# Hedgehog attention with a GLU: the attention coefficients of slabs 1 to 3 spread over the features by DMAs through DRAM

The change calls the four slabs 1 to 4; this text counts them from 0, as the code does. "Slabs 1 to 3" are the second to the fourth.

## The chip, the cores and the metric

The kernel runs on one core of a Trainium2 chip. The core has a matrix engine (TensorE, PE in the profile, with its weight loads shown as PEld), a vector engine (VectorE, DVE), an engine for functions of one input (ScalarE, ACT), a general one (GpSimd, POOL) and SyncE (SP), which here only issues DMAs. The metric is the device time of one execution, in microseconds.

## The reference

The input is one sequence of 2048 tokens with 512 features. Two layers of the same weights follow one another, each a linear attention and a GLU, with a layernorm before and a residual after each. All is bfloat16.

```python
def _A_ref(x, wqkv, w_phi, wo):          # H = 32 heads, Dh = 16
    q, k, v = ...                        # from x @ wqkv, per head
    pq = jnp.einsum("bhsd,hdf->bhsf", q, w_phi)
    pk = jnp.einsum("bhsd,hdf->bhsf", k, w_phi)
    phi_q = jnp.concatenate([_softmax(pq, axis=-1), _softmax(-pq, axis=-1)], axis=-1)
    phi_k = jnp.concatenate([_softmax(pk, axis=-1), _softmax(-pk, axis=-1)], axis=-1)
    kv = jnp.einsum("bhsf,bhsd->bhfd", phi_k, v)
    z  = jnp.einsum("bhsf->bhf", phi_k)
    num = jnp.einsum("bhqf,bhfd->bhqd", phi_q, kv)
    den = jnp.einsum("bhqf,bhf->bhq", phi_q, z)[..., None] + 1e-6
    return (num / den) ... @ wo

def _B_ref(x, W_gate, W_up, W_down):     # F = 1376
    gate = x @ W_gate
    return (gate * (gate > 0) * (x @ W_up)) @ W_down

for _ in range(2):
    x = x + _A_ref(_layernorm(x), A_wqkv, A_w_phi, A_wo)
    x = x + _B_ref(_layernorm(x), B_W_gate, B_W_up, B_W_down)
```

## The kernel before

The 2048 tokens are worked in four slabs of 512 (st = 0 to 3), each of four tiles of 128. x stays in on-chip memory as x_sb for the whole run. Queries, keys and what follows from them lie with features on the 128 partitions and the slab's 512 tokens along the free axis. The 512 query features make four chunks c of 128 (8 heads of 16), and each chunk exists for two signs sg, exp(pq) and exp(-pq): eight pieces of 128 x 512 per slab, in expq.

into_a is a layernorm and the keys of a slab (lines 425 to 512). Per tile it makes the exponentials of the keys (expk), their sums per head (L486, L488) and, on POOL, the values weighted by them (vhat, L495). expk and vhat have NE buffers, one per tile. The sums over tokens (kvsum, matmuls with expk and vhat) of a slab run after its four tiles: each sum reads all four buffers. In the first stage the four slabs' into_a follow one another; later into_a(st) follows glu(st), for the next layer.

out_of_a is queries, attend and a layernorm. The two softmaxes of a query and the division by the denominator come down to one coefficient per token, head and sign. attend(st) computes it in these steps:

- 32 small matmuls (L550, bank zd) give per token, head and sign the sum of the exponentials and its part of the denominator.
- ACT copies the sums out (Zs, L553), DVE multiplies and adds (zm L555, zden L557), ACT takes the reciprocal by a logarithm and an exponential (L558, L559), and DVE makes the coefficients atok (L561), with tokens on the partitions.
- PE transposes atok (L565) and DVE copies the result to aT (L566): 64 rows, one for each head and sign, with 512 tokens.
- Per chunk and sign, a matmul of aT with the 0/1 matrix EC (L570) spreads 8 rows of aT over 128 partitions, each row 16 times, into a PSUM bank. DVE multiplies expq by it: for sg = 0 straight from PSUM (L578), for sg = 1 after ACT has copied it to absb (L574, then L575). VIA chooses between the two.
- Two matmuls per chunk (L582) give the attention's output, ACT copies it to oT (L583), 16 matmuls with wo_sb project it (L588) and residual adds the result to x_sb (L592).

glu(st) (L594) has 88 matmuls for gate and up, and 44 with Wd; ACT takes the ReLU (L607), DVE multiplies (L609) into hT, which has NH slots; one glu holds 11 of them until its last tile is projected.

The order written in the code is, per layer: sums(); out_of_a(0); then for st = 0 to 3: out_of_a(st + 1), glu(st), and into_a(st) or, in the second layer, four output stores (L648).

That is not the order in which the engines run it. Program.schedule (L119) is a planner that runs at build time. Each operation has an engine, a cost occ (how long it holds its engine) and a latency lat. The planner takes the operation that can start first by these costs, and of several the one written first. The result is one fixed list per engine; a semaphore wait stands before an operation where it needs another engine's result. On the chip nothing is reordered: when an operation's input is late, all that is behind it on its engine waits.

A DMA is planned by these lines: it holds its issuer for 0.56 us on SP, all DMAs share one transfer line of 270 bytes per ns, and a fixed latency lies partly before and partly after.

```python
DMA_LAT = 1800.0
DMA_BW = 270.0
...
begin = max(s + 0.35 * self.DMA_LAT, qfree)
qfree = begin + o.nbytes / self.DMA_BW
o.finish = qfree + 0.65 * self.DMA_LAT
```

So nbytes, given with each DMA, sets only its planned time; what is moved is set by the access patterns. Operations with port=True (L575 and the layernorm's apply L449) are planned not to overlap with POOL's arithmetic.

Before the change the only DMAs after the loads at the start are the 16 output stores. They wait for one another, since all write the resource "out".

Of the kernel before, what the change touches and what calls it, by code (L numbers as in the profile page):

```python
# [7 lines left out]
BF16 = mybir.dt.bfloat16  # L8
I32 = mybir.dt.int32
ALU = mybir.AluOpType  # L10
ACT = mybir.ActivationFunctionType
# [47 lines left out]
class Program:  # L59
# [10 lines left out]
    def op(self, eng, fn, reads=(), writes=(), occ=100.0, lat=None, name="", bonus=0.0, port=False):  # L70
        o = Op(len(self.ops), eng, fn, reads, writes, occ, occ + 100.0 if lat is None else lat, name)
        o.bonus, o.port = bonus, port
        self.ops.append(o)
        return o
# [172 lines left out]
def build_kernel(nc, A_x, A_wqkv, A_w_phi, A_wo, W_gate, W_up, W_down, out):  # L247
# [8 lines left out]
    with ExitStack() as ctx:  # L256
# [4 lines left out]
        def sb(name, shape, dt=BF16):  # L261
            return E(nc.sbuf_tensor(name, [P] + list(shape), dt))

        NWARM = 8
        NY, NYT, NE, NV, NG, NH, NA = 4, 6, 6, 4, 3, 19, 3
        x_sb = sb("x_sb", [NT, 512])
        ytile = sb("ytile", [NY, 512])
        yT = sb("yT", [NYT, NC, 512])
# [33 lines left out]
        ident = sb("ident", [128])  # L302
        mask8a = sb("mask8a", [8])
        mask8 = sb("mask8", [8])
        absb = sb("absb", [NA, 512])
        pb = [E(nc.psum_tensor(f"pb{i}", [P, 512], FP32)) for i in range(8)]

        made = {}
# [1 line left out]
        def R(*key):  # L310
            if key not in made:
                made[key] = Res(str(key))
            return made[key]
# [3 lines left out]
        def bank(name):  # L317
            return Bank(name, pb)

        def mm(ps, view, lhsT, rhs, start, stop, reads, n, name):  # L320
            lat = 0.4167 * n + 167
            op("pe", lambda e: e.matmul(view(ps), lhsT, rhs, start=start, stop=stop),  # L322
               reads=reads, writes=[ps], occ=max(25.0, 0.4167 * n + 2.6), lat=lat, name=name)
# [5 lines left out]
        def full(ps):  # L329
            return ps.f32()  # L330

        def b16half(ps):
            return ps.b16()[:, 0:512]
# [85 lines left out]

        fold("k", Wknat, Wkp)  # L420

        cnt = {"y": 0, "yT": 0, "e": 0, "h": 0, "g": 0, "v": 0, "a": 0}
        VIA = lambda st, c, sg: sg == 1

        def layernorm(st, step=4, early=False):

# [112 lines left out]
        def attend(st):  # L539

            g = st % 2
            zd = bank(f"zd{st}")

            def zdv(p):
                return p.f32().rearrange("p (t q s h) -> p t q s h", t=4, q=2, s=2)

            for tt in range(4):
                for sg in range(2):
                    for c in range(NC):
                        mm(zd, (lambda tt, sg, c: lambda p: zdv(p)[:, tt, :, sg, c * 8:(c + 1) * 8])(tt, sg, c),  # L550
                           expq[:, st, c, sg, tt * 128:(tt + 1) * 128], ZDw[:, sg, c, :].rearrange("p (q h) -> p q h", q=2), True, True,
                           [R("eq", st, c, sg), R("ZDw", sg, c), R("ZDw1")], 16, f"zd{st}")
            op("act", lambda e: e.activation(Zs[:, g], zdv(zd)[:, :, 0], ACT.Copy), reads=[zd], writes=[R("Zs", g)], occ=270, lat=400, name="Zs")  # L553
            for s in range(2):
                op("dve", (lambda s: lambda e: e.tensor_tensor(zm[:, g, :, s, :], zdv(zd)[:, :, 1, s], Zs[:, g, :, 1 - s, :], ALU.mult))(s),  # L555
                   reads=[zd, R("Zs", g)], writes=[R("zm", g, s)], occ=200, lat=290, name="zm")
            op("dve", lambda e: e.tensor_tensor(zden[:, g], zm[:, g, :, 0, :], zm[:, g, :, 1, :], ALU.add), reads=[R("zm", g, 0), R("zm", g, 1)], writes=[R("zden", g)], occ=200, lat=290, name="zden")  # L557
            op("act", lambda e: e.activation(zr[:, g], zden[:, g], ACT.Ln), reads=[R("zden", g), R("tables")], writes=[R("zr", g)], occ=200, lat=300, name="zln")  # L558
            op("act", lambda e: e.activation(zr[:, g], zr[:, g], ACT.Exp, scale=-1.0), reads=[R("zr", g)], writes=[R("zr", g)], occ=200, lat=300, name="zr")  # L559
            for s in range(2):  # L560
                op("dve", (lambda s: lambda e: e.tensor_tensor(atok[:, g, :, s * 32:(s + 1) * 32], Zs[:, g, :, 1 - s, :], zr[:, g], ALU.mult))(s),  # L561
                   reads=[R("Zs", g), R("zr", g)], writes=[R("atok", g)], occ=195, lat=290, name="atok")
            pa = bank(f"aT{st}")
            for tt in range(4):
                tr(pa, (lambda tt: lambda p: p.b16()[:, tt * 128:(tt + 1) * 128])(tt), atok[:, g, tt, :], [R("atok", g)], f"aTt{st}")  # L565
            op("dve", lambda e: e.tensor_copy(aT[:, g, :], b16half(pa)), reads=[pa], writes=[R("aT", g)], occ=328, lat=415, name="aT")  # L566
            for c in range(NC):
                for sg in range(2):
                    ps = bank(f"ab{st}{c}{sg}")
                    mm(ps, full, EC[:, sg * 4 + c, :], aT[:, g, :], True, True, [R("EC"), R("aT", g)], 512, f"ab{st}")  # L570
                    if VIA(st, c, sg):
                        ab = cnt["a"] % NA
                        cnt["a"] += 1
                        op("act", (lambda ab, ps: lambda e: e.activation(absb[:, ab, :], full(ps), ACT.Copy))(ab, ps), reads=[ps], writes=[R("absb", ab)], occ=480, lat=610, name=f"abc{st}")  # L574
                        op("dve", (lambda c, sg, ab: lambda e: e.tensor_tensor(expq[:, st, c, sg, :], expq[:, st, c, sg, :], absb[:, ab, :], ALU.mult))(c, sg, ab),  # L575
                           reads=[R("eq", st, c, sg), R("absb", ab)], writes=[R("eq", st, c, sg)], occ=335, lat=420, name=f"em{st}", port=True)
                    else:
                        op("dve", (lambda c, sg, ps: lambda e: e.tensor_tensor(expq[:, st, c, sg, :], expq[:, st, c, sg, :], full(ps), ALU.mult))(c, sg, ps),  # L578
                           reads=[R("eq", st, c, sg), ps], writes=[R("eq", st, c, sg)], occ=595, lat=690, name=f"em{st}")
                pn = bank(f"num{st}{c}")  # L580
                for sg in range(2):
                    mm(pn, full, kvbd[:, sg, c, :], expq[:, st, c, sg, :], sg == 0, sg == 1, [R("kvbd", sg, c), R("eq", st, c, sg)], 512, f"num{st}")  # L582
                op("act", (lambda c, pn: lambda e: e.activation(oT[:, g, c, :], full(pn), ACT.Copy))(c, pn), reads=[pn], writes=[R("oT", g, c)], occ=480, lat=610, name=f"oT{st}")  # L583
            for tt in range(4):
                t = 4 * st + tt
                ps = bank(f"wo{t}")
                for c in range(NC):
                    mm(ps, full, oT[:, g, c, tt * 128:(tt + 1) * 128], wo_sb[:, c, :], c == 0, c == NC - 1, [R("oT", g, c), R("wo")], 512, f"wo{t}")  # L588
                residual(t, ps)
# [116 lines left out]
```

## Time and profile before

| | |
|---|---|
| median of 3 runs | 429.52 us (429.41 to 431.32) |
| the profiled execution's own time | 429.99 us |
| its span, first to last instruction | 428.2 us |
| DVE busy | 283.2 us (66% of the span) |
| ACT busy | 222.4 us (52%) |
| granted PE clock, mean of the span | 0.999 of full speed |
| L570 spreading matmuls | 64 (8 slabs of 8) |
| L574 copies to absb | 32, mean 620 ns |
| L566 copies to aT, when | 70.7, 71.4, 87.9, 164.8 us; 274.7, 275.4, 324.4, 360.9 us |

The spans of instructions are taken by the hardware profiler in one execution. Matmuls are pipelined: a single one lasts some 380 ns from start to end by the profile, but the next one starts before it ends, so the pace of a row of matmuls is read from their starts. "Idle before" is time in which an engine did nothing before an instruction, put down to what released it. The first of the eight L566 copies belongs to slab 0 of the first layer; the second four belong to the second layer.

### The profile page before, as it was taken

What the parts mean: (1) busy time and instruction counts of PE and PEld (TensorE: products, weight loads), DVE (VectorE), ACT (ScalarE), POOL (GpSimd) and SP (SyncE); (2) the same over time, 40 slices, a digit from 0 to 9 for tenths busy, and PEclk for the clock granted to TensorE, in tenths of its full rate; (3) what the DMA queues carried; (4) which work ended last, traced back from release to release, by engine and by line L of the source; (5) the groups of instructions that cost most, each with busy time, mean ns of one, the idle gap of its engine ahead of it and who ended that gap; (6) DMA issues with size and microseconds to landing.
All of it is one profiled execution on the core that took longest, in us unless ns stands there. A gap on an engine that the chain in (4) does not pass through costs nothing.

```text
span 428.2 us, 6499 instructions
## 1 busy us (share of the span) xinstructions
PE 414.4 (97%) x2521; PEld 210.3 (49%) x2568; DVE 283.2 (66%) x590; ACT 222.4 (52%) x452; POOL 69.2 (16%) x71
## 2 busy tenths in 40 slices
PE   8899999899999999999999999989999999999997
PEld 4455555445455445454445445534444444444443
DVE  6989768994589548883774446888536834843332
ACT  6999888655084515742183169865514422450320
POOL 0439670000007000610052007000000000000000
PEclk9999999999999999999999999999999999999999
DMA  8940000000000000000000000000000001000001
GB/s 269 383 139 2 2 0 2 2 0 2 0 2 2 0 0 2 0 2 0 2 0 2 1 2 0 2 2 0 2 24 27 0 1 51 0 2 27 22 2 49
DMA packets 9598, 10.95 MB, mean 26 GB/s; under 512 B 1024, under 2 KB 8544, under 8 KB 9568
## 3 DMA queue, kind: packets, MB, share of 16 engines
q1 hardware_dynamic: 9024, 10.01, 6.9%
q10 hardware_dynamic: 544, 0.52, 0.4%
q8 instruction: 20, 0.33, 0.3%
q14 instruction: 10, 0.08, 0.1%
HBM read 8.44 MB, written 2.10 MB: 25 GB/s over the span
## 4 chain that ended last, share of the span: by engine, by line
PE 85%; ACT 9%; DVE 4%; issue 1%; POOL 0%
PE pb L322 80%; PE pb L326 3%; ACT expk L484 3%; ACT ytile L446 2%; DVE x_sb L592 1%; ACT vsb L492 1%; DVE stats L432 1%; ACT expq L536 1%; PE pb L377 1%; DVE expq L578 1%; ACT Wqp L417 0%; ACT hT L406 0%; ACT yT L460 0%; DVE Wkp L414 0%; ACT oT L583 0%
## 5 line engine op out<-in xcount | busy, mean ns | idle before, releaser
L607 ACT ACTIVATE gate_sb<-pb 128x512 bf16<-128x512 f32 (+1 forms) x88 | 52.8, 599 | 145.3 <-PE pb L322 143.9
L495 POOL TENSOR_TENSOR vhat<-vsb,rZk 128x544 bf16<-128x544 bf16 x64 | 68.4, 1102 | 196.0 <-DVE rZk L488 182.0
L609 DVE TENSOR_TENSOR hT<-gate_sb,pb 128x512 bf16<-128x512 bf16 (+1 forms) x88 | 59.9, 684 | 60.6 <-PE pb L322 60.4
L322 PE MATMUL pb<-yT,Wu 128*128 128x512 bf16 (+1 forms) x348 | 92.1, 379 | 0.1
L322 PE MATMUL pb<-yT,Wg 128*128 128x512 bf16 (+1 forms) x340 | 90.4, 379 | 0.7
L322 PE MATMUL pb<-Wd,hT 128*128 128x512 bf16 (+1 forms) x344 | 77.0, 379 | 0.4
L592 DVE TENSOR_TENSOR x_sb<-x_sb,pb 128x512 bf16<-128x512 bf16 x64 | 41.9, 685 | 47.6 <-PE pb L322 47.5
L322 PEld LDWEIGHTS pb<-Wd,hT 128*128 128x128 bf16 (+1 forms) x352 | 34.4, 98 | 41.5
L322 PEld LDWEIGHTS pb<-yT,Wu 128*128 128x128 bf16 (+1 forms) x352 | 35.1, 100 | 38.8
L322 PEld LDWEIGHTS pb<-yT,Wg 128*128 128x128 bf16 (+1 forms) x352 | 34.5, 100 | 36.7
L486 DVE TENSOR_REDUCE Zk<-expk 128x64 f32<-128x1024 bf16 x32 | 38.4, 1202 | 13.3 <-ACT expk L484 13.1
L432 DVE BATCH_NORM_STATS2 stats<-x_sb 128x6 f32<-128x512 bf16 x64 | 42.5, 678 | 0.8 <-DMA x_sb<-in_A_x_dram 0.3
L536 ACT ACTIVATE expq<-pb 128x512 bf16<-128x512 f32 x64 | 35.3, 702 | 12.8 <-PE pb L322 12.8
L484 ACT ACTIVATE expk<-pb 128x512 bf16<-128x512 f32 x64 | 37.1, 667 | 3.6 <-PE pb L322 2.3
L322 PE MATMUL pb<-wv,yT 128*128 128x512 bf16 x126 | 33.7, 379 | 0.3
L322 PE MATMUL pb<-wo_sb,oT 128*128 128x512 bf16 x126 | 33.5, 379 | 0.2
L322 PE MATMUL pb<-Wkp,yT 128*128 128x512 bf16 x122 | 32.1, 379 | 1.3 <-ACT yT L460 0.9
L322 PE MATMUL pb<-yT,Wqp 128*128 128x512 bf16 x121 | 30.9, 379 | 0.5 <-issue 0.2
L460 ACT ACTIVATE yT<-pb 128x512 bf16<-128x512 bf16 x52 | 27.3, 609 | 3.3 <-PE pb L326 3.3
L322 PE MATMUL pb<-vhat,expk 128*128 128x136 bf16 x256 | 24.3, 223 | 1.0 <-POOL vhat L495 0.8
L322 PE MATMUL pb<-expq,kvbd 128*128 128x512 bf16 x59 | 20.7, 380 | 3.3 <-DVE expq L575 3.0
L574 ACT ACTIVATE absb<-pb 128x512 bf16<-128x512 f32 x32 | 17.8, 620 | 11.6 <-PE pb L322 11.6
(63 smaller groups left out, 375.0 us busy)
## 6 DMA issues: line engine op xcount, KB each, us to landing
out_dram<-x_sb SPq DMA_DIRECT2D x16, 128.0 KB, 1.7
x_sb<-in_A_x_dram SPq DMA_DIRECT2D x3, 512.0 KB, 8.5
Wg<-in_B_W_gate_dram SPq DMA_DIRECT2D x1, 1376.0 KB, 10.6
Wu<-in_B_W_up_dram SPq DMA_DIRECT2D x1, 1376.0 KB, 13.6
Wd<-in_B_W_down_dram SPq DMA_DIRECT2D x1, 1280.0 KB, 15.7
hT<-in_A_wqkv_dram ACTq DMA_DIRECT2D x2, 256.0 KB, 3.5
wv<-in_A_wqkv_dram SPq DMA_DIRECT2D x1, 512.0 KB, 5.3
hT<-in_A_wqkv_dram SPq DMA_DIRECT2D x1, 512.0 KB, 7.6
```

Source lines behind the costliest of these rows:

```text
L322: op("pe", lambda e: e.matmul(view(ps), lhsT, rhs, start=start, stop=stop), reads=reads, writes=[ps], occ=max(25.0, 0.4167 * n + 2.6), lat ...
L326: op("pe", lambda e: e.transpose(view(ps), src, ident[:]), reads=list(reads) + [R("ident")], writes=[ps], occ=56, lat=220, name=name)
L432: op("dve", (lambda t: lambda e: e.bn_stats(stats[:, t, :], x_sb[:, t, :]))(t), reads=[R("x", t)], writes=[R("st", t)], occ=580, lat=680, ...
L460: op("act", (lambda ps, dst: lambda e: e.activation(dst, b16half(ps).rearrange("p (c n) -> p c n", c=NC), ACT.Copy))(ps, dst), reads=[ps], ...
L484: op("act", (lambda i, s, pk: lambda e: e.activation(expk[:, i, s, :], full(pk), ACT.Exp, scale=1.0 - 2.0 * s))(i, s, pk), reads=[pk], wri ...
L486: op("dve", (lambda i, zb: lambda e: e.tensor_reduce(Zk[:, zb, :], expk[:, i, :, :].rearrange("p s (h f) -> p (s h) f", f=16), AX.X, ALU.a ...
L495: op("pool", (lambda i, s, vb, rz: lambda e: e.tensor_tensor(vhat[:, i, s, :, :], vsb[:, vb, :, :], rZk[:, rz, s * 32:(s + 1) * 32].unsque ...
L536: op("act", (lambda c, s, ps: lambda e: e.activation(expq[:, st, c, s, :], full(ps), ACT.Exp, scale=1.0 - 2.0 * s))(c, s, ps), reads=[ps], ...
L574: op("act", (lambda ab, ps: lambda e: e.activation(absb[:, ab, :], full(ps), ACT.Copy))(ab, ps), reads=[ps], writes=[R("absb", ab)], occ=4 ...
L592: op("dve", lambda e: e.tensor_tensor(x_sb[:, t, :], x_sb[:, t, :], full(ps), ALU.add), reads=[R("x", t), ps], writes=[R("x", t)], occ=597 ...
L607: op("act", (lambda m, gb, pg: lambda e: e.activation(gate_sb[0:m, gb, :], pg.f32()[0:m, :], ACT.Relu))(m, gb, pg), reads=[pg], writes=[R( ...
L609: op("dve", (lambda m, gb, hb, pu: lambda e: e.tensor_tensor(hT[0:m, hb, :], gate_sb[0:m, gb, :], pu.f32()[0:m, :], ALU.mult))(m, gb, hb, pu),
```

## The change

For slabs 1 to 3 of each layer the matmuls with EC are gone. aT, 64 rows of 512 tokens, is stored to DRAM by one DMA (64 KB, into one of two scratch tensors), and eight DMAs read it back, one for each chunk and sign. Each reads eight rows of 1 KB, every row 16 times, and so fills abT[:, gi, :], 128 partitions of 512 tokens. All nine are issued by SP; the reads wait for the store to be complete. DVE then multiplies expq by abT for both signs. Slab 0 is worked as before, with its ACT copies going to the odd places of abT in place of absb. abT has one buffer for each of the eight pieces, so a read waits until the slab before has used that piece.

The rows of aT are put in the order of the chunks (chunk, sign, head in place of sign, chunk, head), so that a piece's eight rows lie together; atok is written, and EC indexed, in that order. For each read the planner is told 350000 bytes; the read writes 131072. To make room, the key buffers NE go from 6 to 5 and the slots NH of hT from 19 to 18; absb goes.

```diff
@@ -262,7 +262,7 @@
             return E(nc.sbuf_tensor(name, [P] + list(shape), dt))
 
         NWARM = 8
-        NY, NYT, NE, NV, NG, NH, NA = 4, 6, 6, 4, 3, 19, 3
+        NY, NYT, NE, NV, NG, NH = 4, 6, 5, 4, 3, 18
         x_sb = sb("x_sb", [NT, 512])
         ytile = sb("ytile", [NY, 512])
         yT = sb("yT", [NYT, NC, 512])
@@ -302,7 +302,8 @@
         ident = sb("ident", [128])
         mask8a = sb("mask8a", [8])
         mask8 = sb("mask8", [8])
-        absb = sb("absb", [NA, 512])
+        abT = sb("abT", [8, 512])
+        scratch = [nc.dram_tensor(f"spread{i}", (64, 512), BF16, kind="Internal").ap() for i in range(2)]
         pb = [E(nc.psum_tensor(f"pb{i}", [P, 512], FP32)) for i in range(8)]
 
         made = {}
@@ -419,8 +420,8 @@
 
         fold("k", Wknat, Wkp)
 
-        cnt = {"y": 0, "yT": 0, "e": 0, "h": 0, "g": 0, "v": 0, "a": 0}
-        VIA = lambda st, c, sg: sg == 1
+        cnt = {"y": 0, "yT": 0, "e": 0, "h": 0, "g": 0, "v": 0, "s": 0}
+        VIA = lambda c, sg: sg == 1
 
         def layernorm(st, step=4, early=False):
 
@@ -558,25 +559,35 @@
             op("act", lambda e: e.activation(zr[:, g], zden[:, g], ACT.Ln), reads=[R("zden", g), R("tables")], writes=[R("zr", g)], occ=200, lat=300, name="zln")
             op("act", lambda e: e.activation(zr[:, g], zr[:, g], ACT.Exp, scale=-1.0), reads=[R("zr", g)], writes=[R("zr", g)], occ=200, lat=300, name="zr")
             for s in range(2):
-                op("dve", (lambda s: lambda e: e.tensor_tensor(atok[:, g, :, s * 32:(s + 1) * 32], Zs[:, g, :, 1 - s, :], zr[:, g], ALU.mult))(s),
+                op("dve", (lambda s: lambda e: e.tensor_tensor(atok[:, g, :, 0:64].rearrange("p t (c s h) -> p t c s h", s=2, h=8)[:, :, :, s, :], Zs[:, g, :, 1 - s, :].rearrange("p t (c h) -> p t c h", h=8),
+                                                               zr[:, g].rearrange("p t (c h) -> p t c h", h=8), ALU.mult))(s),
                    reads=[R("Zs", g), R("zr", g)], writes=[R("atok", g)], occ=195, lat=290, name="atok")
             pa = bank(f"aT{st}")
             for tt in range(4):
                 tr(pa, (lambda tt: lambda p: p.b16()[:, tt * 128:(tt + 1) * 128])(tt), atok[:, g, tt, :], [R("atok", g)], f"aTt{st}")
             op("dve", lambda e: e.tensor_copy(aT[:, g, :], b16half(pa)), reads=[pa], writes=[R("aT", g)], occ=328, lat=415, name="aT")
+            if st:
+                scr = scratch[cnt["s"] % 2]
+                cnt["s"] += 1
+                rs = R("scr", cnt["s"] % 2)
+                dma("sp", lambda e: e.dma_start(scr, aT[0:64, g, :]), reads=[R("aT", g)], writes=[rs], nbytes=65536, name=f"aTo{st}")
+                for gi in range(8):
+                    dma("sp", (lambda gi: lambda e: e.dma_start(abT[:, gi, :], scr[8 * gi:8 * gi + 8, :].unsqueeze(1).to_broadcast([8, 16, 512])))(gi),
+                        reads=[rs], writes=[R("abT", gi)], nbytes=350000, name=f"abT{st}")
             for c in range(NC):
                 for sg in range(2):
-                    ps = bank(f"ab{st}{c}{sg}")
-                    mm(ps, full, EC[:, sg * 4 + c, :], aT[:, g, :], True, True, [R("EC"), R("aT", g)], 512, f"ab{st}")
-                    if VIA(st, c, sg):
-                        ab = cnt["a"] % NA
-                        cnt["a"] += 1
-                        op("act", (lambda ab, ps: lambda e: e.activation(absb[:, ab, :], full(ps), ACT.Copy))(ab, ps), reads=[ps], writes=[R("absb", ab)], occ=480, lat=610, name=f"abc{st}")
-                        op("dve", (lambda c, sg, ab: lambda e: e.tensor_tensor(expq[:, st, c, sg, :], expq[:, st, c, sg, :], absb[:, ab, :], ALU.mult))(c, sg, ab),
-                           reads=[R("eq", st, c, sg), R("absb", ab)], writes=[R("eq", st, c, sg)], occ=335, lat=420, name=f"em{st}", port=True)
-                    else:
+                    gi = 2 * c + sg
+                    if st == 0:
+                        ps = bank(f"ab{st}{c}{sg}")
+                        mm(ps, full, EC[:, gi, :], aT[:, g, :], True, True, [R("EC"), R("aT", g)], 512, f"ab{st}")
+                    if st == 0 and not VIA(c, sg):
                         op("dve", (lambda c, sg, ps: lambda e: e.tensor_tensor(expq[:, st, c, sg, :], expq[:, st, c, sg, :], full(ps), ALU.mult))(c, sg, ps),
-                           reads=[R("eq", st, c, sg), ps], writes=[R("eq", st, c, sg)], occ=595, lat=690, name=f"em{st}")
+                           reads=[R("eq", st, c, sg), ps], writes=[R("eq", st, c, sg)], occ=597, lat=690, name=f"em{st}")
+                        continue
+                    if st == 0:
+                        op("act", (lambda gi, ps: lambda e: e.activation(abT[:, gi, :], full(ps), ACT.Copy))(gi, ps), reads=[ps], writes=[R("abT", gi)], occ=480, lat=610, name=f"abc{st}")
+                    op("dve", (lambda c, sg, gi: lambda e: e.tensor_tensor(expq[:, st, c, sg, :], expq[:, st, c, sg, :], abT[:, gi, :], ALU.mult))(c, sg, gi),
+                       reads=[R("eq", st, c, sg), R("abT", gi)], writes=[R("eq", st, c, sg)], occ=335, lat=425, name=f"em{st}", port=True)
                 pn = bank(f"num{st}{c}")
                 for sg in range(2):
                     mm(pn, full, kvbd[:, sg, c, :], expq[:, st, c, sg, :], sg == 0, sg == 1, [R("kvbd", sg, c), R("eq", st, c, sg)], 512, f"num{st}")

```

## The prediction

> **What bounds the kernel now.** I read the page first: busy shares, the slices, the chain that ended last.
>
> ```profile
> PE 414.4 (97%) x2521; PEld 210.3 (49%) x2568; DVE 283.2 (66%) x590; ACT 222.4 (52%) x452; POOL 69.2 (16%) x71
> ...
> PE   8899999899999999999999999989999999999997
> ...
> PE 85%; ACT 9%; DVE 4%; issue 1%; POOL 0%
> ```
>
> TensorE (PE) is busy 97% of the span and carries 85% of the chain. So first ask how much PE time goes, then whether PE stays fed. The second view is the busy time by stretch (columns: stretch, its length, then per engine busy us and instructions, PE first).
>
> ```profile
> 71.00:88.00 17.00, 15.60 (x114) 8.05 (x114) 16.05 (x43) 13.36 (x30) 0.00 (x0) 1.00 0.00 1
> 275.00:293.40 18.40, 16.18 (x110) 7.25 (x110) 16.06 (x42) 13.79 (x31) 0.00 (x0) 1.00 0.00 1
> 100.00:120.00 20.00, 19.89 (x93) 9.20 (x93) 10.61 (x18) 4.57 (x9) 0.00 (x0) 1.00 0.00 0
> 320.00:340.00 20.00, 19.89 (x104) 9.49 (x105) 14.43 (x31) 8.19 (x16) 0.00 (x0) 1.00 0.06 21
> ```
>
> In 100 to 120 us and in 320 to 340 us PE lacks 0.11 us of 20: full. In two other stretches it isn't: 71 to 88 us, 1.40 us idle, and 275 to 293.4 us, 2.22 us. I call them gap A and gap B. They are the start of the two layers, where slab 1's attention is worked beside slab 0's because the first GLU can't begin before slab 0's layernorm. The timeline of PE shows it in A (start, duration, line, operands, count, idle time before):
>
> ```profile
> 82.14 0.38 PE L322 MATMUL pb<-wo_sb,oT 128*128 128x512 bf16 x1
> 83.25 0.39 PE L322 MATMUL pb<-expq,kvbd 128*128 128x512 bf16 x1 [0.73 <-DVE expq L575]
> 84.25 0.39 PE L322 MATMUL pb<-expq,kvbd 128*128 128x512 bf16 x1 [0.61 <-DVE expq L575]
> ...
> 87.75 1.03 PE L322 MATMUL pb<-yT,Wg 128*128 128x512 bf16 x4
> ```
>
> PE waits twice for L575 products of slab 1, and the first gate matmul (Wg) starts at 87.75. The same in B, where it starts at 293.34:
>
> ```profile
> 288.29 0.39 PE L322 MATMUL pb<-expq,kvbd 128*128 128x512 bf16 x1 [1.65 <-DVE expq L575]
> ...
> 293.34 0.59 PE L322 MATMUL pb<-yT,Wg 128*128 128x512 bf16 x2
> ```
>
> **Part 1, what goes.** The spreading matmuls (L570) of slabs 1 to 3, eight per slab and two layers: 48. A group of eight in a full stretch gives the price:
>
> ```profile
> 115.63 2.54 PE L322 MATMUL pb<-Wd,hT 128*128 128x512 bf16 x11
> 118.01 1.89 PE L322 MATMUL pb<-aT,EC 128*128 128x512 bf16 x8
> 119.74 0.38 PE L322 MATMUL pb<-expq,kvbd 128*128 128x512 bf16 x1
> ```
>
> From 118.01 to 119.74 eight matmuls pass: 1.73 us, 0.216 each (the 381 ns below is one matmul's latency; they overlap). 48 x 0.216 = 10.4 us. With them go 24 L574 copies on ScalarE (ACT), paced 0.48 us: 11.5 us of an engine busy 52%, behind PE in the full stretches, so costed at nothing; without that cover they would be a gain.
>
> ```profile
> L578 DVE TENSOR_TENSOR expq<-expq,pb 128x512 bf16<-128x512 bf16 x32 | 21.4, 682 | 1.4 <-PE pb L322 1.4
> ...
> L322 PE MATMUL pb<-aT,EC 128*128 128x512 bf16 x63 | 17.1, 381 | 0.1
> L575 DVE TENSOR_TENSOR expq<-expq,absb 128x512 bf16<-128x512 bf16 x32 | 13.1, 422 | 0.0
> ```
>
> The 24 L578 products from PSUM become L575 products from SBUF: 682 against 422 ns, in sequence 0.60 against 0.33, so VectorE (DVE) is relieved of 24 x 0.27 = 6.5 us. In the full stretches PE hides that too. It matters only in the gaps.
>
> **Part 2, what is added on SP's queue.** Six stores of 64 KB and 48 reads that write 128 KB each. No row shows a read that repeats a row, so I bound it by these:
>
> ```profile
> q1 hardware_dynamic: 9024, 10.01, 6.9%
> ...
> out_dram<-x_sb SPq DMA_DIRECT2D x16, 128.0 KB, 1.7
> ...
> x_sb<-in_A_x_dram SPq DMA_DIRECT2D x2, 128.0 KB, 3.0
> ```
>
> Arrival, counted from the aT copy. Store: 1.7 us (the 128 KB row). Issue on SP: 0.37 us for the first output store at 317.38, 1.4 us for the 1376 KB weight loads. Landing: 1.7 us (store) to 3.0 us (128 KB loads in the crowded start). Last of eight reads: between 1.7 + 0.2 + 7 x 0.37 + 1.7 = 6.2 us and 1.7 + 0.2 + 7 x 1.4 + 3.0 = 14.7 us. The packets allow it: q1's 6.9% of 16 x 428.2 us over 9024 packets is 52 ns each, so 128 packets on 16 engines take 0.42 us, less than the issue.
>
> [...]
>
> What the planner believes, from the code: store 0.12 + 0.63 + 0.24 + 1.17 = 2.2 us; a read costs 350000/270 = 1.30 us of transfer; the first is there at 0.12 + 0.63 + 1.30 + 1.17 later, 5.4 us after aT, the eighth at 5.4 + 7 x 1.30 = 14.5 us. I take the lower arrival (the row of equal size): data are there before the planned turn, and DVE doesn't wait on them. Only the slow end is late, by 0.2 us. A late product would hold behind it, on DVE, slab 0's residual adds and statistics in the gaps, or L609's products in a GLU, and PE behind these.
>
> **Part 3, where the order moves.** After aT, slabs 1 to 3 now have up to 14.5 us before their last product. For slabs 2 and 3 a GLU covers it: 132 matmuls x 0.216 = 28.5 us. Closest is slab 3 of the second layer: aT at 360.9, glu(3) about 28.9 us (the same 132 at 0.219) before the end at 428, so at 399. Coefficients plus the 15 us that products, projection and layernorm take today (360.9 to the transposes at 375.7) end near 390. That fits. Four of six slabs give their 8 x 0.216 in full: 6.9 us. In the second layer the output stores stand on the same queue (each waits for its forerunner, 1.4 us at most); the reads are hidden by the same GLU, and the stores at the end have nothing new before them.
>
> Slab 1 is different: its work is what fills the gaps. Gap A today: PE does 8 + 8 spreading, 8 + 8 L582 and 16 + 12 projection matmuls (60 x 0.216 = 13.0 us) and some small ones. Afterwards:
> The way to glu(0) shortens. DVE has slab 0's products alone: 4 x 0.60 + 4 x 0.33 = 3.7 us from 71.75, so 75.5; then L582, the copy L583 (0.63) and a projection matmul: first residual add at 76.9 instead of 77.8. Four adds and four statistics at 0.60 + 0.66: 81.9. Logarithm, exponential and their waits 0.9: the apply at 82.8 instead of 84.1. Apply 0.4, transposes 0.3, four ACT copies paced 0.48: first Wg near 85.6, against 87.75.
> What PE has in these 85.6 - 71.2 = 14.4 us: slab 0's 32 matmuls 6.9, 30 small L550 ones 1.2, transposes 1.1, and of slab 1 some six L582 matmuls 1.3 (its first products come at 77.2 by plan, and DVE is busy for slab 0 until 82). Sum 10.5, idle 3.9 instead of 1.4: +2.5 us.
> Gap B alike: add at 281.0 instead of 282.18, apply at 287.0 instead of 288.74, first Wg near 289.7. 14.6 us with 10.5 of work: 4.1 idle instead of 2.2, +1.9 us. Together +4.4. Bounds: 0, if the planner finds other fillers, and 12.1, if the gaps end when they do now and hold nothing of slab 1 (28 matmuls x 0.216 = 6.05 each).
>
> **Part 4, the smaller buffers.** NE from 6 to 5: key tile 2 of the next slab must wait until the sums of the last have read all four buffers. Today the third tile stops there. In slab 2 of the first stage those sums end at 41.84; tile 2's exponentials (40.37) would move to 41.9, its GpSimd products from 44.3 to 45.5, and of that delay 0.7 us falls into the idle time before 47.20: 0.5 us stays. Bounds 0 (other work fills PE) and 2.2 (one tile's two L495 at 1.1). I take 0.5. NH from 19 to 18 costs nothing: a GLU holds 11 slots, and the next one's first products come when its forerunner's last projection is done (Wg at 323.83 after Wd to 323.6); without that cover, one L609 of 0.60. The new order of heads in atok and EC moves no instruction.
>
> **Sum**, against the profiled execution's 429.99 us (span 428.2 and 1.8 around it): -10.4 + 4.4 + 0.5 = -5.5, so 424.5. That execution lies 0.47 above the median of 429.52, so **424.0 us**.
>
> **Rivals.**
> Full gain: the gaps don't grow and the buffers cost nothing, 429.5 - 10.4 = 419.1 us. For it: DVE is busy 16.05 of 17 us in A and is relieved there. Against: PE then needs 4 us of other work in the gaps, and the query matmuls, today's other filler, all start before 70.4 and 274.6.
> Slower, the gaps: slab 1's coefficients come by plan when slab 0's layernorm holds DVE, all of slab 1 slides behind the gap, and glu(0) starts no sooner. Idle +12.1, buffers +0.5: 429.5 - 10.4 + 12.6 = 431.7 us. It decides from the point where the gaps together gain over 9.9 us of idle time. For it: L575's waits on PE today, 1.3 and 1.6 us, are slab 1's late products already. Against: the chain through slab 0 loses three of slab 1's products on DVE.
> Late transfers: all at the slow end, the store at 3.0 us too, the last read comes after 14.7 + 1.3 = 16.0 us, 1.5 late. In the two gaps alone that makes 424.0 + 3.0 = 427.0; if each of the six slabs passes it on to PE, 424.0 + 9.0 = 433.0. Against: the planned 14.5 us lies above nearly the whole bound, and a GLU leaves DVE idle time (60.4 us before L609 in all).
>
> **How the numbers follow.** About 0.5% (2.15 us) can be told from no change here. Forecast 0.60 (own range 421.5 to 427.3), full gain 0.15, late transfers 0.10 (half of it under 431.7, half over), gaps 0.12, and 0.03 for something between forecast and gaps. So faster 0.75, same 0.05 + 0.03 = 0.08, slower 0.12 + 0.05 = 0.17. The range reaches from full gain almost to the slower case and leaves out some 0.18: 419 to 430.5.
>
> **What would show it.** PE matmuls pb<-aT,EC: 16 instead of 64. Idle PE time from slab 0's aT copy to the first Wg: near 4 us in each layer, with Wg some 2 to 3 us sooner after that copy. The other stretches as full as now. No DVE product waits for a DMA into abT by more than a few tenths; the eighth read lands 6 to 10 us after the aT copy. The forecast falls if glu(1) to glu(3) show idle PE, or if a gap holds over 6 us.

## The result, and the profile after

The changed kernel takes 427.81 us (median of 20 runs, 425.73 to 429.93) against 429.88 us before (20 runs, 429.41 to 431.32): a ratio of 0.9948, 95% interval 0.9936 to 0.9961. That is 2.1 us faster, where 5.5 us were forecast. The direction held, the size did not, and the scatter of the changed kernel is about twice that of the one before.

The profiled execution took 427.66 us, with these lines on its page (span, busy times, PE's busy tenths and the granted clock in tenths, by 40 slices):

```profile
span 425.9 us, 6489 instructions
...
PE 410.3 (96%) x2520; PEld 207.2 (49%) x2520; DVE 276.6 (65%) x590; ACT 211.3 (50%) x428; POOL 69.3 (16%) x71
...
PE   7899999799999999999999999969999999999995
...
PEclk9999999889999999999999999998999999999999
```

The last line is new. Before, the clock stood at 9 in all slices; now it falls to 8 in three of them. PE's busy line has a 7 and a 6 there or just before, where it had 8s. The stretches that the prediction looked at, in the same view (columns: stretch, length, busy time and instructions of PE, PEld, DVE, ACT and POOL, granted clock, DMA share, GB/s):

```profile
71.00:88.00 17.00, 14.09 (x92) 6.68 (x91) 13.83 (x38) 9.42 (x22) 0.00 (x0) 0.81 0.21 71
275.00:293.40 18.40, 14.97 (x98) 7.13 (x97) 14.85 (x40) 11.29 (x26) 0.00 (x0) 0.91 0.18 61
100.00:120.00 20.00, 20.00 (x97) 9.30 (x95) 11.62 (x25) 4.89 (x9) 0.00 (x0) 1.00 0.01 1
320.00:340.00 20.00, 20.00 (x97) 9.21 (x96) 9.21 (x18) 5.87 (x10) 0.00 (x0) 1.00 0.22 76
```

Gap A has 2.91 us of idle PE time instead of 1.40, gap B 3.43 instead of 2.22, and the mean clock in them is 0.81 and 0.91 instead of 1.00. The full stretches stay full. PE's timeline, gap A first, then gap B:

```profile
78.86 1.04 PE L323 MATMUL pb<-wo_sb,oT 128*128 128x512 bf16 x4
82.79 1.89 PE L323 MATMUL pb<-expq,kvbd 128*128 128x512 bf16 x4 [2.89 <-DVE expq L589]
...
89.44 1.03 PE L323 MATMUL pb<-yT,Wg 128*128 128x512 bf16 x4
```

```profile
282.52 0.78 PE L323 MATMUL pb<-ZDw,expq 128*128 128x16 bf16 x25
286.43 1.89 PE L323 MATMUL pb<-expq,kvbd 128*128 128x512 bf16 x4 [3.13 <-DVE expq L589]
288.12 0.63 PE L323 MATMUL pb<-wo_sb,oT 128*128 128x512 bf16 x1
...
292.15 0.38 PE L323 MATMUL pb<-yT,Wg 128*128 128x512 bf16 x1
```

In each gap PE stands still once for some 3 us, waiting for L589, a product of slab 1 on DVE. What follows is slow: from 286.43 to 288.12 four matmuls pass, 0.42 us each, where such a row took 0.216 before. The clock by single microseconds in gap A says why:

```profile
80.00:81.00 1.00, 0.00 (x0) 0.00 (x0) 1.00 (x3) 0.00 (x0) 0.00 (x0) 1.00 0.00 0
81.00:82.00 1.00, 0.00 (x0) 0.00 (x0) 1.00 (x5) 0.00 (x0) 0.00 (x0) 0.74 0.00 0
82.00:83.00 1.00, 0.21 (x1) 0.10 (x1) 1.00 (x5) 0.14 (x1) 0.00 (x0) 0.50 0.00 0
83.00:84.00 1.00, 1.00 (x3) 0.31 (x3) 1.00 (x4) 0.50 (x3) 0.00 (x0) 0.50 0.00 0
...
86.00:88.00 2.00, 2.00 (x13) 1.19 (x11) 0.79 (x4) 0.81 (x2) 0.00 (x0) 0.50 0.13 33
88.00:90.00 2.00, 2.00 (x13) 1.15 (x12) 0.00 (x0) 1.82 (x5) 0.00 (x0) 0.92 0.15 46
```

PE is empty from 79.9 on. At about 81.5, 1.6 us into the idle stretch, the granted clock falls to 0.50, and it stays there to about 88.3, 5.5 us after PE has work again. Busy time times what the clock withholds, summed over single microseconds, is some 2.8 us in gap A and some 1.6 us in gap B (there from 286.3 to 289.7): about 4.3 us in all.

The transfers, on SP's queue: the store of slab 1's aT at 70.06, and eight reads in a row:

```profile
70.06 0.52 SPq L573 DMA_DIRECT2D spread<-aT  x1
72.06 5.05 SPq L575 DMA_DIRECT2D abT<-spread  x8
```

While they run, from 74 to 79 us, the mean busy share of the DMA engines is 0.51 to 0.56, at 176 to 192 GB/s (the last two columns); the loads at the start show a share of 1.10, at 348 GB/s:

```profile
73.00:74.00 1.00, 0.98 (x9) 0.40 (x8) 0.71 (x2) 1.00 (x3) 0.00 (x0) 1.00 0.24 82
...
76.00:77.00 1.00, 1.00 (x11) 0.53 (x10) 0.77 (x3) 0.60 (x1) 0.00 (x0) 1.00 0.53 185
...
79.00:80.00 1.00, 0.90 (x4) 0.20 (x2) 1.00 (x3) 0.38 (x1) 0.00 (x0) 1.00 0.21 74
...
10.00:12.00 2.00, 0.55 (x5) 0.34 (x6) 1.99 (x6) 2.00 (x7) 0.00 (x0) 1.00 1.10 348
```

The data of the eighth read are moving until about 79.5, 9.5 us after the aT copy ended at 70.03. DVE waits for a transfer only twice in the whole run by more than 0.1 us, the longer time in slab 3 of the first layer, the other time in gap B, just ahead of slab 0's residual adds:

```profile
170.26 0.42 DVE L589 TENSOR_TENSOR expq<-expq,abT 128x512 bf16<-128x512 bf16 x1 [1.50 <-DMA abT<-spread]
...
279.62 0.43 DVE L589 TENSOR_TENSOR expq<-expq,abT 128x512 bf16<-128x512 bf16 x1 [0.69 <-DMA abT<-spread]
```

One more line matters, the last residual add:

```profile
421.60 0.69 DVE L603 TENSOR_TENSOR x_sb<-x_sb,pb 128x512 bf16<-128x512 bf16 x1 [1.69 <-PE pb L323]
```

It ends at 422.29 and the span at 425.9, 3.6 us later. Before, that was 428.2 less 426.06, 2.1 us. The end of the program has become 1.5 us longer.

So the 2.3 us by which the span is shorter come together like this: 10.4 us of matmuls gone; 2.7 us more idle PE time in the gaps; 4.3 us for the clock; 1.5 us at the end. These make 1.9 us less; the remaining 0.4 us were not traced.

### The profile page after: what moved, and what is told of

The parts are those of the page before. It is cut to its first block, busy times and chain, and to the rows that moved or that the text cites. A ratio compares the mean times of both kernels' runs of the same rounds, so it can differ in the third digit from the quotient of the medians.

```text
span 425.9 us, 6489 instructions
## 1 busy us (share of the span) xinstructions
PE 410.3 (96%) x2520; PEld 207.2 (49%) x2520; DVE 276.6 (65%) x590; ACT 211.3 (50%) x428; POOL 69.3 (16%) x71
## 4 chain that ended last, share of the span: by engine, by line
PE 85%; ACT 10%; DVE 4%; POOL 1%; issue 0%; POOLq 0%
PE pb L323 80%; PE pb L327 4%; ACT expk L485 2%; ACT expq L537 2%; ACT ytile L447 1%; DVE x_sb L603 1%; DVE stats L433 1%; ACT vsb L493 1%; PE pb L378 1%; POOL vhat L496 1%; ACT Wqp L418 0%; ACT hT L407 0%; ACT oT L594 0%; ACT abT L588 0%; ACT yT L461 0%; DVE Zk L487 0%
## 5 line engine op out<-in xcount | busy, mean ns | idle before, releaser
L323 PE MATMUL pb<-yT,Wg 128*128 128x512 bf16 (+1 forms) x352 | 94.1, 379 | 0.1
L323 PE MATMUL pb<-Wd,hT 128*128 128x512 bf16 (+1 forms) x352 | 78.4, 379 | 0.0
L323 PE MATMUL pb<-wo_sb,oT 128*128 128x512 bf16 x128 | 35.6, 392 | 0.2 <-ACT oT L594 0.2
L323 PE MATMUL pb<-Wkp,yT 128*128 128x512 bf16 x128 | 33.3, 379 | 0.9 <-ACT yT L461 0.9
L323 PE MATMUL pb<-yT,Wqp 128*128 128x512 bf16 x128 | 32.9, 379 | 0.5 <-ACT Wqp L418 0.5
L594 ACT ACTIVATE oT<-pb 128x512 bf16<-128x512 f32 x32 | 18.8, 621 | 22.6 <-PE pb L323 22.5
L323 PE MATMUL pb<-expq,kvbd 128*128 128x512 bf16 x64 | 22.7, 410 | 6.0 <-DVE expq L589 6.0
```

## The experiments

All were timed beside runs of the kernel before on the same chip. The ratio is to these, so small differences between sessions (429.9 to 430.3 us for the kernel before) drop out.

| run | median, us | ratio to before (95%) | mean clock, profiled execution |
|---|---|---|---|
| changed kernel | 427.81 | 0.9948 (0.9936 to 0.9961) | 0.988 |
| e1_last_wait_order | 427.23 | 0.9927 (0.9910 to 0.9945) | 0.988 |
| e2_fill_gaps | 424.71 | 0.9871 (0.9858 to 0.9884) | 1.000 |
| e3_before_small_buffers | 433.13 | 1.0066 (1.0053 to 1.0078) | 0.996 |
| e4_from_slab2 | 426.94 | 0.9924 (0.9910 to 0.9938) | 0.992 |
| e5_fill_and_one_wait | 423.15 | 0.9836 (0.9824 to 0.9849) | 1.000 |
| e6_true_bytes | 428.34 | 0.9947 (0.9928 to 0.9967) | 0.991 |
| e7_six_key_buffers | 434.42 | 1.0104 (1.0086 to 1.0121) | 0.980 |
| e8_from_slab2_six | 429.23 | 0.9988 (0.9974 to 1.0002) | 0.992 |
| e9_before_fill | 430.91 | 1.0019 (1.0010 to 1.0028) | 1.000 |
| e10_small_buffers_fill | 431.42 | 1.0033 (1.0020 to 1.0045) | 0.999 |
| e11_from_slab2_fill | 424.61 | 0.9870 (0.9856 to 0.9885) | 1.000 |
| e12_true_bytes_fill | 425.15 | 0.9898 (0.9876 to 0.9920) | 1.000 |

### The clock: fillers in the gaps

```diff
                 residual(t, ps)
+            if st == 0:
+                wb = bank(f"warm{st}")
+                for tt in range(1, 4):
+                    for k in range(4):
+                        mm(wb, full, EC[:, 0, :], aT[:, g, :], True, True,
+                           [R("EC"), R("aT", g), R("x", tt)], 512, "fill")
```

Twelve matmuls per layer into a bank that nobody reads. Each four wait for a residual add of slab 0, so they land in the idle stretch.

> The changed kernel with 12 more matmuls per layer whose results nobody reads, placed in the idle stretch of PE behind slab 0's residual adds; nothing else moves. Theory (clock): a single idle stretch of about 3 us is what halves the granted PE clock, which costs 2.8 us in gap A and 1.6 us in gap B; with the stretch cut to about 1 us the clock stays at 1.0 in both gaps and the time falls by 3 to 4.5 us, to about 424 us, and the spread of the runs shrinks. Rival (the gaps are set by DVE's and ACT's chain, and the clock costs nothing there): the clock may stay up, but the time stays within 0.7 us of 427.8, or rises by up to 24 x 0.216 = 5.2 us.

Measured 424.71 us (424.34 to 424.94), ratio 0.9871: 3.1 us faster than the changed kernel, and the runs now lie within 0.6 us. The stretches of gap A in this run:

```profile
80.00:81.00 1.00, 1.00 (x6) 0.42 (x5) 1.00 (x3) 0.00 (x0) 0.00 (x0) 1.00 0.01 2
81.00:82.00 1.00, 1.00 (x6) 0.49 (x5) 1.00 (x4) 0.00 (x0) 0.00 (x0) 1.00 0.00 0
82.00:83.00 1.00, 0.68 (x4) 0.10 (x1) 1.00 (x5) 0.00 (x0) 0.00 (x0) 1.00 0.00 0
...
86.00:88.00 2.00, 2.00 (x16) 1.08 (x15) 1.14 (x5) 2.00 (x5) 0.00 (x0) 1.00 0.13 32
```

PE has work at 80 us, where it had none, and the clock stays at 1.00. Idle PE time in the gaps falls too, which is no gain in itself (the fillers are not useful work). The theory of the clock holds, within its 3 to 4.5 us.

Another order is not the reason. Apart from the fillers, the traces show the same instructions in the same order on ScalarE, GpSimd and SyncE as in the changed kernel, and on VectorE too but for the place of one semaphore wait. The 20 executions of the changed kernel also say the same without any filler: one with a mean clock of 0.996 took 425.73 us, three with 0.992 took 426.79 in the median, nine with 0.988 took 427.79 and seven with 0.986 took 428.33. From the first to the third of these that is 0.26 us for each 0.001 of clock; carried on to 1.000 it gives an estimate of 424.7 us, the time of the run with the fillers.

The control is the same edit in the kernel before. In its profiled execution the clock needs no help. In others it does: of the 55 executions of that kernel beside these runs, 33 have a mean clock of 0.995 or 0.996 (median 430.34 us), 22 have 0.999 or 1.000 (429.73 us).

> Control: the kernel before with the same 12 filler matmuls per layer. There the clock is at 1.0 in both gaps without them. Theory (the fillers help the changed kernel only by keeping the clock up): no gain here, between 0 and 24 x 0.216 = 5.2 us slower than before, most likely 0 to 2, since part of them falls into idle time. Rival (the fillers help by something else, say by another order of the other engines): faster than before by over 1 us here too.

430.91 us against 430.11 for its neighbours, ratio 1.0019: 0.8 us slower, and 1.2 us slower than the eight of those 16 neighbours whose clock stayed up (429.75). The fillers as such bring nothing. The control is not quite the same edit, though: here the planner also put DVE's and ACT's work in another order, so the 0.8 us are not the price of the fillers alone.

### The end of the program

The order of the last waits, and in later runs a single wait:

```diff
-            for s in range(N_DSEM):
+            last = [o.stream for o in self.seq["sp"] if o.is_dma][-1]
+            for s in [(last + 1 + i) % N_DSEM for i in range(N_DSEM)]:
                 if self.count[s]:
                     eng.wait_ge(dsems[s], 16 * self.count[s])
```

There are 60 semaphores and 86 DMAs now, so the last store has number 25 and 34 waits stood behind it. Before, 32 DMAs left the last store's wait as the last one.

> The changed kernel with one edit: SP's waits for its DMA semaphores at the end stand in another order, that of the last DMA last. Theory (end of the program): the span behind the last residual add grew from 2.2 to 3.6 us because 34 of 60 such waits now stand behind the wait for the last output store, so this run should be some 1.4 us faster than the changed kernel (about 426.4 against 427.8 us), and the span should end some 2.2 us after the last add. Rival (the last store itself lands later than before): no change, 427.8 us, and still 3.6 us.

427.23 us; by the ratios 0.9927 and 0.9948 that is 0.9 us faster, with intervals that overlap a little. In its profile the span ends 2.7 us after the last add (425.4 less 422.74), instead of 3.6. By the profile that is most of the 1.5 us, not all, and the trace shows why: SyncE's waits are recorded from 423.15 to 424.91, one every 0.06 us without a pause, and these 1.8 us are longer than the 1.7 us that a store of 128 KB takes. In the changed kernel the same row stops once for the store, until 424.07, and then goes on to 425.46. With one wait and the fillers:

> The changed kernel with the 12 filler matmuls per layer, and at its end one wait only, for the last output store (the others are implied: the stores wait for one another, and every load and read has been waited for by its user). Theory (clock and end add up): 424.7 for the fillers less 1.4 for the end, about 423.3 us, clock 1.0, and about 2.2 us from the last add to the end of the span. Rival (one of the two hides the other): 424.7 us.

423.15 us, ratio 0.9836, 1.6 us below the fillers alone. The last add of this run:

```profile
418.34 0.69 DVE L607 TENSOR_TENSOR x_sb<-x_sb,pb 128x512 bf16<-128x512 bf16 x1 [1.69 <-PE pb L322]
```

It ends at 419.03 and the span at 421.2: 2.2 us, as before the change. Clock and end add up as expected, and this is the fastest version found: 1.6% faster than the kernel before, and it beats the changed kernel by 4.7 us.

### The smaller buffers

```diff
-        NY, NYT, NE, NV, NG, NH, NA = 4, 6, 6, 4, 3, 19, 3
+        NY, NYT, NE, NV, NG, NH, NA = 4, 6, 5, 4, 3, 18, 3
```

> The kernel before with NE 5 instead of 6 and NH 18 instead of 19, and nothing else. The prediction's step: 0.5 us slower than before (bounds 0 and 2.2). Rival, from the changed kernel's slab 0 copy of aT coming 1.8 us sooner than before: the smaller buffers cost nothing, or even gain up to 1.8 us through another order of the first stage.

433.13 us, 2.8 us slower than its neighbours (ratio 1.0066). That is above the prediction's upper bound of 2.2. The key tile that the prediction named is held up a little (its first GpSimd product starts at 44.92 instead of 44.30), but the stage makes up for it: slab 0's aT copy comes sooner (69.55 instead of 70.68). The loss lies in the gaps. Gap A holds less work: the 32 small L550 matmuls that PE did between 70 and 83 us before are now at 165 to 170 us. PE in gap A of this run waits in one piece, where the kernel before waited 0.73 and 0.61:

```profile
80.92 0.40 PE L326 MATMUL pb<-ident,atok 128*128 128x128 bf16 x4
83.64 0.79 PE L322 MATMUL pb<-expq,kvbd 128*128 128x512 bf16 x2 [2.33 <-DVE expq L578]
```

and in gap B the clock goes:

```profile
289.00:290.00 1.00, 0.00 (x0) 0.00 (x0) 1.00 (x5) 0.23 (x1) 0.00 (x0) 1.00 0.00 0
290.00:291.00 1.00, 0.78 (x2) 0.19 (x3) 1.00 (x4) 0.67 (x3) 0.00 (x0) 1.00 0.00 0
...
292.00:293.00 1.00, 1.00 (x5) 0.41 (x3) 1.00 (x3) 0.60 (x1) 0.00 (x0) 0.50 0.00 0
...
294.00:295.00 1.00, 0.97 (x10) 0.72 (x9) 0.60 (x3) 0.67 (x2) 0.00 (x0) 0.69 0.00 0
```

PE is idle for 1.24 us until 290.00 and for 0.20 us before 291.00; then the clock is at 0.50 from 291.2 to 294.6, which is 1.6 us of PE's time. With the fillers:

> The kernel before with NE 5 and NH 18 and the filler matmuls. Without them it was 2.8 us slower than before, of which 1.6 us by the records were the clock in gap B and 1.6 us idle time. Theory: the fillers bring the clock part back and nothing of the idle time, about 431.5 us (433.1 less 1.6); clock 1.0. Rival (the small buffers cost their time elsewhere): 433 us or more with the clock at 1.0.

431.42 us, as expected, with the clock at 0.999 on average and at 1.00 in the gaps: 1.7 us come back, 1.4 us against its own neighbours (ratio 1.0033) stay. The cut between clock and idle time is not clean, since DVE and ACT have another order here than without the fillers. Against the kernel before with the same fillers (430.91 us, ratio 1.0019) only 0.5 us stay, with intervals that overlap. So what the smaller buffers cost with the clock held up lies between 0.5 and 1.4 us.

### Which slabs

Here slab 1 is worked by matmuls, as before the change, and the last wait stands last. (In the lines that choose between matmuls and transfers, the tests for slab 0 become tests for slabs 0 and 1.)

```diff
-            if st:
+            if st > 1:
...
-                    if st == 0:
+                    if st < 2:
```

> The changed kernel with slab 1 spread by matmuls as before, only slabs 2 and 3 through DRAM, and the last wait last. Theory (slab 1's own matmuls are what feeds PE in the gaps; the loss is there): gaps as before the change with about 1.4 and 2.2 us idle and the clock at 1.0, and 32 x 0.216 = 6.9 us less than before: about 423 us. Rival (the transfers cost time wherever they are): 425 us or more, with idle PE in the GLUs.

426.94 us and the clock at 0.5 for 3.4 us in each layer: a miss. The buffers of NE 5 are still in it, and alone in the kernel before they already made the clock fall in gap B. What it does say: with and without slab 1's transfers (427.23 and 426.94) the time is the same within 0.3 us. With the fillers the clock is out of it:

> Slab 1 by matmuls, slabs 2 and 3 through DRAM, NE 5 and NH 18, the fillers and one wait at the end. It tells what slab 1's transfers are worth once the clock stays up (against 423.15 with all three slabs through DRAM and the same two edits). Theory (the gaps last as long as slab 0's chain on DVE and ACT, and PE has room in them for slab 1's 16 spreading matmuls): the same within 1 us, 422.5 to 424. Rival (PE bound there too): 16 x 0.216 = 3.5 us more, 426.6.

424.61 us, against 423.15 with all three slabs. Slab 1's transfers are then worth 1.5 us out of the 3.5 us of matmuls they remove, a little more than the theory allowed: the gaps have room for some of these matmuls, not for all.

### Six key buffers again

```diff
-        NY, NYT, NE, NV, NG, NH = 4, 6, 5, 4, 3, 18
+        NY, NYT, NE, NV, NG, NH = 4, 5, 6, 4, 3, 18
```

> The changed kernel with six key buffers again (NE 6), paid for with one buffer of yT (NYT 5 instead of 6), and one wait at the end. Theory (the smaller key buffers change the first stage's order, and that widens the gaps: they cost 2.8 us in the kernel before): idle time in gap A falls from 2.9 to under 2 us, the clock stays up there, about 423.5 us. Rival (with slab 1's coefficients late the gaps stay as they are whatever the buffers): 426.4 us, clock at 0.5 in both.

> Slab 1 by matmuls, slabs 2 and 3 through DRAM, six key buffers with NYT 5, one wait at the end. Theory (slab 1's transfers and the small buffers are the whole loss): gaps as in the kernel before, clock 1.0, 32 x 0.216 = 6.9 us less than before: about 423 us. Rival (something else in slabs 2 and 3 costs): 425 us or more with the clock at 1.0.

434.42 and 429.23 us: both miss their theory. The memory was taken from yT, and that made a new idle stretch before slab 0's coefficients, in both layers. In the second of the two runs, in single microseconds:

```profile
275.00:276.00 1.00, 0.06 (x4) 0.00 (x0) 0.65 (x3) 0.70 (x3) 0.00 (x0) 1.00 0.00 0
276.00:277.00 1.00, 0.26 (x4) 0.17 (x4) 0.58 (x2) 1.00 (x5) 0.00 (x0) 1.00 0.00 0
277.00:278.00 1.00, 0.99 (x31) 0.99 (x32) 0.78 (x3) 0.43 (x2) 0.00 (x0) 0.69 0.00 0
278.00:279.00 1.00, 1.00 (x9) 0.59 (x6) 1.00 (x5) 0.38 (x1) 0.00 (x0) 0.50 0.00 0
```

1.7 us of idle time, in two pieces of 1.07 and 0.62 us, are enough here: the clock halves at about 277.4, when PE has just resumed. So these runs say nothing on NE itself; that six key buffers would help the changed kernel, if their memory came from elsewhere, is left open.

### The longer transfer times of the plan

```diff
-                        reads=[rs], writes=[R("abT", gi)], nbytes=350000, name=f"abT{st}")
+                        reads=[rs], writes=[R("abT", gi)], nbytes=131072, name=f"abT{st}")
```

> The changed kernel with the reads told to the planner with the 131072 bytes that they write instead of 350000, and one wait at the end. Theory (the long planned transfers are what pushes slab 1's products behind slab 0's layernorm and leaves PE idle): products of slab 1 stand earlier on DVE, less than 2 us of idle PE in each gap, the clock up for most of them, about 423 to 424 us. Rival (DVE has no room for them before the statistics in any case): the gaps stay at about 3 us with the clock at 0.5, 426.4 us (427.8 less the end); a third case, the reads come later than so planned and DVE stands still for them: over 427 us, with waits for abT over 1 us.

428.34 us. The clock fell in both gaps, for 3.4 us in each, and DVE stood still for abT in 14 places, 8.6 us in all; the third case, then, with part of the rival. In slab 3 of the second layer:

```profile
369.70 0.43 DVE L588 TENSOR_TENSOR expq<-expq,abT 128x512 bf16<-128x512 bf16 x1 [0.27 <-DMA abT<-spread]
370.39 0.43 DVE L588 TENSOR_TENSOR expq<-expq,abT 128x512 bf16<-128x512 bf16 x1 [0.27 <-DMA abT<-spread]
371.09 0.42 DVE L588 TENSOR_TENSOR expq<-expq,abT 128x512 bf16<-128x512 bf16 x1 [0.27 <-DMA abT<-spread]
```

Three reads in a row arrive 0.70 us apart, while this plan reckons 0.56 (SP's issue). With the clock kept up:

> As the run with fillers and one wait at the end (423.15 us), but with the reads told to the planner with their true 131072 bytes. It tells what the longer planned times are worth once the clock stays up. Theory (with true bytes DVE stands still for reads that come later than planned, 8.6 us over the whole run where the clock was not held up, and PE waits behind it): clock at 1.0 and 1 to 3 us slower, 424.2 to 426. Rival (the loss of the true bytes was the clock alone): 423.2 us.

425.15 us against 423.15: the longer planned times are worth 2.0 us by the medians, 2.7 us by the ratios; the six runs scatter over 3.2 us. DVE waited 7.6 us for abT here, and 1.9 us with the 350000 bytes.

## Why the prediction was right in direction and wrong in size

**Part 1** held. The pace of 0.216 us and the 48 matmuls make 10.4 us, and PE's busy time less the clock's share fell by that: 417.9 - 1.6 in the small-buffer version of the kernel before (all matmuls recorded), 410.3 - 4.3 in the changed one, 10.3 us.

**Part 2** held in what it needed. The last read ended 9.5 us after the aT copy, inside the 6.2 to 14.7 us, but not at the lower end that was taken. The row of equal size (1.7 us) was the wrong one: the store took 1.9, the first read 3.1 us from issue (167.19 to DVE's start at 170.26), and the reads took some 0.7 us each (128 KB at 176 to 192 GB/s), at a mean share of 0.51 to 0.56 of the DMA engines, where the prediction reckoned 0.42 us from its packets on all 16. The upper end of its "6 to 10 us" for the eighth read rests on no run; measured were those 9.5 us. Since the plan reckoned 14.5 us, it cost little: 2.2 us of DVE waits, though both, 1.5 and 0.7 us, are more than the few tenths allowed for.

**Part 3, the gaps**, is the step that failed: "Sum 10.5, idle 3.9 instead of 1.4: +2.5 us", and the same in B, with all PE work after the idle time at the full pace. The idle time itself came smaller than forecast (+1.5 and +1.2 us instead of +2.5 and +1.9). What was missing is the clock: 4.3 us by the records, 3.1 us by the run with the fillers, because behind idle stretches of 2.9 and 3.1 us the granted clock was 0.50, for 6.8 and 3.4 us, and what ran in that time is slab 0's transposes and slab 1's projection, on the way to the first gate matmul. The prediction had looked at a profile in which the clock never moved, and took it for constant. It also forecast the first Wg 2 to 3 us sooner after the aT copy; it came 3.5 us later in A (20.55 us instead of 17.07) and 0.3 us sooner in B (18.38 instead of 18.67). In A the last ACT copy of slab 0 was planned behind three oT copies, so the adds began 8.5 us after aT instead of 7.1; the other 2.1 us of the delay come later. In B the adds (281.0) and the apply (287.4) came near where the forecast had them, but by luck: the aT copy had come 0.9 us sooner (273.77), and from there the adds took 7.2 us instead of the 6.3 forecast, behind an atok product that waited 0.68 us for ACT. That slabs 2 and 3 give all of their matmuls held: their stretches have no idle time but 0.43 us at 179.

**Part 4, the buffers**: 0.5 us was mis-sized; alone in the kernel before they cost 2.8 us, 1.6 of it by the clock in the records; with the clock held up 0.5 to 1.4 us stay. The mechanism was wrong too. The key tile lost 0.6 us and the stage made it up; what cost time was the planner's new order. It took the small L550 matmuls out of gap A; what it changed on the way to gap B was not traced.

**The end**: "the stores at the end have nothing new before them" was true and beside the point: the prediction added nothing for the end. Something new stands behind them, 34 waits for semaphores, 1.5 us in the profile, of which 0.9 us (with intervals that overlap) and in a second form 1.6 us were taken back.

Of the rivals, the full gain is out. Late transfers are out, with those 2.2 us in the whole run and PE full behind the longer wait. The rival in which the gaps swallow the gain came closest: they did so, 7.0 of 10.4 us, though by the clock more than by idle time and below its turning point.

## What to carry to other kernels

Price idle time of TensorE in one piece and not only in sum: look whether the granted clock can fall behind it (here it did with 1.4 to 3.1 us of idle time), and add half of the PE work that then runs at the lower clock: 1.6 us for 3.4 us at half rate here, 2.8 us for 6.8. Where such a stretch is set by a chain on other engines, throw-away matmuls in it can pay for themselves (24 of them bought 3.1 us here; in the kernel before they brought no gain). When buffers are cut or DMAs added under a planner, look at what the new order leaves for the places that were already thin, and at what the program's end now waits for.

## What the runs showed of the hardware

The granted clock has two values here, 1.00 and 0.50. In the changed kernel the time at 0.50 lasts 6.83 us (81.48 to 88.31) and 3.41 us (286.28 to 289.69), in e3_before_small_buffers 3.41 us (291.21 to 294.62). Of the 15 falls in or before the gaps of seven profiled executions (changed kernel, e1, e3, e4, e6, e7, e8), 12 last 3.4 us and 3 last 6.8 us.

The falls of one execution also stand whole numbers of 3.413 us apart. In the changed kernel, and in e1, e4, e6 and e8 too, the first and the second are 204.8 us apart, 60 times 3.413; the four of e7_six_key_buffers (69.60, 83.26, 277.82 and 294.88) are 4, 57 and 5 times 3.413 us apart. What sets these marks the runs do not show. One piece of 3.41 us is 0.004 of the mean clock (half of 3.41 us in 426), so that executions with 0.996, 0.992 and 0.988 would have one, two and three of them; this is an estimate, and the profiled ones agree with it (e3 0.996, e4 0.992, changed kernel 0.988).

The length of the idle time alone doesn't decide. The clock fell 1.6 us into an idle stretch of 2.9 us (changed kernel, gap A), 3.0 us into one of 3.1 us (gap B), after pieces of 1.07 and 0.62 us (e8_from_slab2_six) and of 1.24 and 0.20 us (e3_before_small_buffers, gap B). So 1.4 to 3.1 us were enough in these four places. It did not fall after 2.3 us in one piece (e3_before_small_buffers, gap A) or after 1.65 us (kernel before, gap B, in the profiled execution). Where the marks lie in the idle time doesn't tell these cases apart either: in that gap A of e3_before_small_buffers one lies at 83.0, an estimate carried back from 291.21 by 61 steps of 3.413 us, and 1.7 us of the 2.3 lie ahead of it, no less than the 1.6 us ahead of the fall in the changed kernel. What decides stays open.

By the estimate of 0.004 a piece the number of pieces varies from run to run: of the changed kernel's 20 runs the fastest, 425.73 us, had a mean clock of 0.996, and the seven with 0.986 took 427.78 to 429.93.
